# Sixteen single loads of the input, and new hand-written orders, in a four-layer attention and gated-MLP kernel

## The chip, the cores and the metric

The kernel runs on one core of a Trainium2 chip, as one launch. The metric is the device time of that launch in microseconds. Before the change the median of three runs is 380.31 us (379.89 to 380.41). The profile that is read here is of one execution of its own, which took 380.59 us; from its first to its last instruction it spans 378.9 us.

The core has five instruction queues that run side by side and meet only through semaphores: TensorE (PE, with its weight loads as PEld), VectorE (DVE), ScalarE (ACT), GpSimd (POOL) and SyncE (SP), which here does nothing but start DMAs.

## The reference

The input x has 2048 tokens of 448 bf16 values. Four layers follow each other, A, B, A, B, each on the layer-normed x and added back to it. Both A layers use the same weights, and so do both B layers.

```python
def _A_ref(x, wqkv, wo):            # 16 heads of 28
    W, dil = 8, 2
    qkv = (x @ wqkv) -> q, k, v     # split by head
    idx = pos[:, None] - off[None, :]          # 8 keys: the token itself and every second one behind it
    logits = einsum(q, k[idx]) * Dh ** -0.5    # masked where idx < 0
    o = einsum(softmax(logits), v[idx])
    return o @ wo
def _B_ref(x, w_gate, w_up, w_down):           # 1792 hidden values
    return ((x @ w_gate) * (x @ w_up)) @ w_down
x = x + _A_ref(_layernorm(x), A_wqkv, A_wo)
x = x + _B_ref(_layernorm(x), B_w_gate, B_w_up, B_w_down)
x = x + _A_ref(_layernorm(x), A_wqkv, A_wo)
x = x + _B_ref(_layernorm(x), B_w_gate, B_w_up, B_w_down)
```

## The kernel before, in words

**Tiling.** x lies in `x_sb` as 16 blocks of 128 tokens; even tokens are blocks 0 to 7 and odd tokens blocks 8 to 15, so that the dilated window becomes a plain window of 8 neighbours. Each layer is cut into chunks of 256 or 512 tokens, and the chunks of the four layers are interleaved (`SEQ`): a chunk of a later layer starts as soon as its tokens are through the earlier one. Matmuls contract over 64 rows and run two at a time on the two halves of the array; the pair is recorded at L355, and its 32-column variant, which is woven between attention matmuls, at L358.

**The start, which the change touches.** A block of x is loaded (L450), its statistics are taken on DVE (`bn`, L592, and `mv`, L594), ACT makes 1/std in two steps (`lnv`, L595, and `rstd`, L597), DVE writes the normalised block (`xn`, L616), and PE transposes it (`Tps`, L631 or L635) into PSUM, from where ACT or DVE copies it (`T`, L642 and L645). Blocks 14 and 15 of the first layer go through a DMA transpose instead (L624). The qkv weights come in three groups: the V weights `WV`, four stage pieces of the Q and K weights (rows of `hT`, which serves as staging space here), and two small pieces `stv` for a packed layout. Eight copies (`wqk`, L517, on DVE or ACT) spread the stage pieces into `WQK`, and every Q/K matmul waits for all eight. After the last Q/K matmul of tokens 0 to 767 four more copies (`wqp`, L525) fill the gaps of `WQK` with V columns, and the Q/K matmuls of the other tokens wait for them. PE runs 18 matmuls on zeros (L509) while it waits for the first data. The evictions of Q/K results (`QK`, L730) and of V results (`V`, `VT`, L795 to L822) may stand on ACT or on DVE.

**What sets the order.** Nothing is scheduled on the chip or by a planner at build time. The table `ORDER` lists for each of the five queues the numbers of the operations in the order in which they are issued (an entry such as `504*2.4.5/475:1+316:2` is an attention operation with pieces of two others woven in), and `BANKS` gives each PE operation its PSUM banks. An operation waits for the semaphores of its producers and for the release of its banks. Which of two engines runs an eviction is also set by the list in which its number stands. `plain_dma` (L450) adds one DMA on SP; `load_x(q, lo, hi)` adds the load of blocks 4q+lo to 4q+hi-1 as one DMA:

```python
def load_x(q, lo=0, hi=4, tag="", prio=0.0):
    two, b0 = q // 2, 4 * (q % 2)
    plain_dma("sp", x_sb[:, 4 * q + lo:4 * q + hi, :], x_par[two][:, b0 + lo:b0 + hi, :], ...)
```

**The MLP weights.** `WGU` holds the gate weights (`wg`) in rows 0 to 63 and the up weights (`wu`) in rows 64 to 127, each loaded in six pieces of which each waits for the one before it. The MLP's pairs compute a gate product and an up product at once (`Gps`); ACT copies the gate half (L1013), DVE multiplies (L1019), and the down product (`Dd`) is added to x (L980). In layers 1 and 3 the transposes are DMA transposes on SP (L621), which the first MLP matmuls wait for.

Of the kernel before, what the change touches and what calls it, by code (L numbers as in the profile page):

```python
# [15 lines left out]
NCH = S // 512  # L16
# [81 lines left out]
def grp_nc(g):  # L98
# [21 lines left out]
    ),  # L120
    "act": (
# [10 lines left out]
    ),  # L132
    "dve": (
# [1028 lines left out]
```

## Time and profile before

| what | us |
|---|---|
| median of three runs | 380.31 |
| the profiled execution | 380.59 |
| its span | 378.9 |
| PE busy | 373.2 (99%) |
| DVE busy | 271.6 (72%) |
| ACT busy | 199.3 (53%) |
| first matmul on real weights starts at | 8.56 |
| first Q/K matmul starts at | 11.86 |
| first MLP matmul starts at | 50.05 |

PE is counted as busy from the start of a matmul to its modelled end, so a busy PE can still be a little slower than its best. The granted TensorE clock is 1.00 in every stretch that was read. A row of the timeline view gives start, length, engine, line, operation, what it writes and reads, shape, how many instructions were merged, and in brackets the idle time before it with what ended it. "SPq" rows are issues of DMAs, not transfers. A group row of the profile gives busy time and mean ns of one, then the engine's idle time before these instructions.

### The profile page before, as it was taken

How to read it: one execution, taken by the hardware profiler on the slowest of the kernel's cores; microseconds unless marked ns; L12 is line 12 of the kernel's file. 1: busy time of each engine (PE TensorE's matmuls, PEld its weight loads, DVE VectorE, ACT ScalarE, POOL GpSimd, SP SyncE). 2: the span in 40 equal slices, each digit the busy share in tenths (PEclk: the TensorE clock that was granted, in tenths of full speed). 3: DMA queues.
4: the chain of work that ended last, by engine and by line, in shares of the span. 5: the costliest groups of instructions: out<-in, count | busy, mean ns of one | idle time of the engine just before them, and what ended most of it. 6: DMA issues, size and time to landing. Idle time of an engine off the chain costs nothing.

```text
span 378.9 us, 14223 instructions
## 1 busy us (share of the span) xinstructions
PE 373.2 (99%) x6372; PEld 208.2 (55%) x6372; DVE 271.6 (72%) x564; ACT 199.3 (53%) x333; POOL 5.2 (1%) x25
## 2 busy tenths in 40 slices
PE   8999999999999999999999999999999999999997
PEld 3554678544544445455766756554455454444864
DVE  6999989988786385867477978528897587275233
ACT  4898786657444565444466413556766544123310
POOL 5000000000000000000000000000000000000000
DMA  7767464610414023022102125220026104103002
GB/s 248 179 139 150 55 185 132 111 23 21 82 22 69 5 55 72 20 48 55 24 10 52 39 43 100 49 51 21 20 32 95 39 3 90 44 2 74 2 13 98
DMA packets 59892, 24.38 MB, mean 64 GB/s; under 512 B 49016, under 2 KB 59704, under 8 KB 59832
## 3 DMA queue, kind: packets, MB, share of 16 engines
q1 hardware_dynamic: 59688, 23.42, 29.0%
q8 instruction: 50, 0.82, 0.9%
q14 instruction: 10, 0.08, 0.1%
q10 hardware_dynamic: 144, 0.06, 0.1%
HBM read 9.04 MB, written 3.50 MB: 33 GB/s over the span
## 4 chain that ended last, share of the span: by engine, by line
PE 92%; ACT 4%; DMA 2%; SPq 1%; DVE 1%; issue 0%; DVEq 0%
PE ps L355 84%; PE ps L358 4%; PE ps L855 2%; ACT qk L730 2%; PE ps L889 2%; DMA hT<-in_A_wqkv_dram 2%; PE ps L1031 1%; SPq L450 1%; ACT E_sb L864 1%; ACT v_sb L822 0%; ACT R_sb L919 0%; ACT R_sb L920 0%; ACT O_sb L900 0%; DVE WQK L517 0%; DVE Qz L841 0%
## 5 line engine op out<-in xcount | busy, mean ns | idle before, releaser
L355 PE MATMUL ps<-xnTb,WGU 64*128 64x512 bf16 (+1 forms) x1902 | 171.6, 332 | 0.8 <-ACT R_sb L920 0.8
L355 PEld LDWEIGHTS ps<-xnTb,WGU 64*128 64x128 bf16 x1902 | 92.2, 94 | 70.3 <-issue 1.5
L1013 ACT ACTIVATE g_sb<-ps 128x512 bf16<-128x512 f32 x112 | 65.8, 596 | 90.7 <-PE ps L355 86.4
L1019 DVE TENSOR_TENSOR hT<-g_sb,ps 128x512 bf16<-128x512 bf16 x112 | 75.1, 681 | 40.1 <-ACT g_sb L1013 38.8
L355 PE MATMUL ps<-WD,hT 64*128 64x448 bf16 x786 | 80.5, 349 | 0.0
L980 DVE TENSOR_TENSOR x_sb<-x_sb,ps 128x448 bf16<-128x448 bf16 x62 | 36.3, 615 | 30.1 <-PE ps L355 29.8
L355 PEld LDWEIGHTS ps<-WD,hT 64*128 64x128 bf16 x786 | 37.7, 94 | 33.7 <-DVE hT L1019 0.2
L355 PE MATMUL ps<-xnTa,WQK 64*128 64x512 bf16 (+1 forms) x496 | 52.6, 353 | 0.5 <-DVE WQK L517 0.2
L864 ACT ACTIVATE E_sb<-ps,shift_sb 128x1024 bf16<-128x1024 f32 (+1 forms) x36 | 37.2, 1068 | 11.7 <-PE ps L855 11.7
L592 DVE BATCH_NORM_STATS2 st<-x_sb 128x6 f32<-128x448 bf16 x64 | 38.2, 618 | 1.4 <-DMA x_sb<-in_A_x_dram 1.2
L355 PEld LDWEIGHTS ps<-xnTa,WQK 64*128 64x128 bf16 x496 | 22.7, 94 | 22.6 <-DVE O_sb L904 1.0
L730 ACT ACTIVATE qk<-ps 128x1024 bf16<-128x1024 f32 (+1 forms) x28 | 25.4, 931 | 17.5 <-PE ps L355 17.1
L616 DVE TENSOR_SCALAR xn_sb<-x_sb,mv,rstd 128x512 bf16<-128x512 bf16 (+1 forms) x64 | 27.6, 455 | 4.9 <-ACT rstd L597 4.9
L871 DVE TENSOR_TENSOR E_sb<-E_sb,MK 128x1024 bf16<-128x1024 bf16 (+1 forms) x36 | 23.4, 658 | 9.0 <-ACT E_sb L864 8.9
L355 PE MATMUL ps<-wo_g,oT 64*128 64x448 bf16 x151 | 26.0, 350 | 0.0
L355 PE MATMUL ps<-WV,xnTa 64*128 64x336 bf16 (+3 forms) x244 | 23.6, 304 | 0.4 <-DMA WV<-in_A_wqkv_dram 0.4
L919 ACT ACTIVATE R_sb<-R_sb 128x960 f32<-128x960 f32 (+1 forms) x18 | 17.3, 961 | 11.4 <-DVE R_sb L918 11.4
L918 DVE STREAM_SHUFFLE R_sb<-O_sb 128x960 f32<-128x960 f32 (+1 forms) x18 | 21.2, 1180 | 0.0
L900 ACT ACTIVATE O_sb<-ps 128x448 f32<-128x448 f32 (+2 forms) x27 | 13.9, 548 | 11.5 <-PE ps L889 11.3
L939 DVE TENSOR_TENSOR oT<-O_sb,R_sb 128x960 bf16<-128x960 f32 (+1 forms) x16 | 17.5, 1095 | 3.2 <-ACT R_sb L920 3.2
L595 ACT ACTIVATE lnv<-mv,eps_sb 128x2 f32<-128x2 f32 (+1 forms) x33 | 9.2, 292 | 20.0 <-DVE mv L594 17.7
L920 ACT ACTIVATE R_sb<-R_sb 128x960 f32<-128x960 f32 (+1 forms) x18 | 17.3, 959 | 0.3
(67 smaller groups left out, 243.2 us busy)
## 6 DMA issues: line engine op xcount, KB each, us to landing
out_dram<-x_sb SPq DMA_DIRECT2D x15, 112.0 KB, 1.8
x_sb<-in_A_x_dram SPq DMA_DIRECT2D x3, 448.0 KB, 7.4
hT<-in_A_wqkv_dram SPq DMA_DIRECT2D x4, 224.0 KB, 5.5
WGU<-in_B_w_gate_dram SPq DMA_DIRECT2D x4, 224.0 KB, 4.1
WGU<-in_B_w_up_dram SPq DMA_DIRECT2D x4, 224.0 KB, 3.8
WD<-in_B_w_down_dram SPq DMA_DIRECT2D x2, 448.0 KB, 4.2
mv_rows<-oT SPq DMA_DIRECT2D x12, 64.0 KB, 1.7
oT<-mv_rows SPq DMA_DIRECT2D x48, 8.0 KB
```

The costliest lines, as they stand in the source:

```text
L355: return lambda E: E.matmul(out(), lhs(), rhs(), start=start, stop=stop)
L592: sc.add("dve", one(lambda E, B=B: E.bn_stats(st6[:, B, :], x_sb[:, B, :]), ("bn", li, B)), 525.0, deps=[("x", li - 1, B)] + ([("xn", li - ...
L616: sc.add("dve", one(lambda E, B=B, dst=dst, src=src: E.tensor_scalar(dst, src, mv[:, B, 0:1], rstd[:, B:B + 1], ALU.subtract, ALU.mult), ( ...
L730: return E.activation(dst, src, ACT.Copy) if hasattr(E, "activation") else E.tensor_copy(dst, src)
L864: return E.activation(E_sb[:, slot, 2 * hp:2 * hp + 2, 0:w], ps[:, b0:b0 + 2, 0:w], ACT.Exp, bias=shift_sb[:, 0:1], scale=SCALE)
L871: return E.tensor_tensor(e, e, MK[:, kind, 0:nc].unsqueeze(1).unsqueeze(1).to_broadcast([128, 2, w // nc, nc]), ALU.min)
L918: sc.add("dve", one(lambda E: E.stream_shuffle(R, Of, [DH] * 32), ("Rs", li, qb)), dve_est(w) + 20.0, deps=[("Oa", li, g)] + prev, prio=prio)
L919: sc.add("act", one(lambda E: E.activation(R, R, ACT.Ln), ("Rl", li, qb)), act_est(w, False), deps=[("Rs", li, qb)], prio=prio)
L939: return E.tensor_tensor(dst, O.rearrange("p d h n -> p h d n"), Rv.rearrange("p d h n -> p h d n"), ALU.mult)
L980: sc.add("dve", one(lambda E: E.tensor_tensor(x_sb[:, B, :], x_sb[:, B, :], ps[:, bk[w], 0:D], ALU.add), ("x", li, B)), dve_est(D), deps=[ ...
L1013: sc.add("act", one(lambda E, gs=gs, bk=bk: E.activation(g_sb[:, gs, :], ps[:, bk[0], :], ACT.Copy), ("G", li, j, f0)), act_est(512), deps ...
L1019: return E.tensor_tensor(hT[:, f0:f0 + nf, hs, 0:nt], v(g_sb[:, gs, :]), v(ps[:, bk[1], :]), ALU.mult)
```

## The change

The input is loaded by sixteen DMAs of one block (112 KB) each; before, there were two of one block, one of two and three of four. The order on SP becomes x blocks 0, 1, 2, 3, 5, 4, 6, 7, then the V weights, then the four stage pieces as before, then block 15, the first gate piece, and blocks 13, 14, 9, 8, 11, 10, 12. Before, the order after the stage pieces was blocks 12 to 15, the first gate piece, blocks 8 to 11. The operations get new numbers (ten more DMAs stand at the front of the list), and `ORDER` and `BANKS` are new throughout: some evictions change between ACT and DVE, and positions change on every engine but POOL. No arithmetic is added or taken away. The tables are cut to their first lines here; what their numbers mean at the places that count is shown below the diff.

```diff
 ORDER = {
     "pe": (
-        "41 42 43 44 45 46 47 48 49 50 51 52 53 54 112 115 55 56 57 58 211 130 212 133 139 241 136 242 205 235 206 236 229 201 230 203 231 202 157 232 199 154 "
+        "51 52 53 54 55 56 57 58 59 60 61 62 63 122 64 65 66 67 125 68 140 221 222 143 251 149 146 252 215 245 216 246 239 211 167 240 241 212 213 242 164 209 "
...
-    sem_names += ["d_x0g", "d_x0h"]
+    sem_names += [f"d_x{q}{t}" for q in range(NCH) for t in "ghi"]
...
     load_x(0, 0, 1, prio=-51.0)
     load_x(0, 1, 2, "g", -49.6)
-    load_x(0, 2, 4, "h", -49.5)
+    load_x(0, 2, 3, "h", -49.5)
+    load_x(0, 3, 4, "i", -49.5)
...
-    load_x(1, prio=-49.3)
+    for i in range(4):
+        load_x(1, i, i + 1, "_ghi"[i] if i else "", -49.3)
...
     for q in range(2, NCH):
-        load_x(q, prio=-48.5 + 0.5 * (q - 2))
+        for i in range(4):
+            load_x(q, i, i + 1, "_ghi"[i] if i else "", -48.5 + 0.5 * (q - 2))
```

On SP, from the start of the program, before. `hT` stands for the stage pieces (and, in the last row, for the two small pieces of V columns).

```order
L450 DMA x_sb<-in_A_x_dram 128x448 x2
L450 DMA x_sb<-in_A_x_dram 128x2x448
L450 DMA x_sb<-in_A_x_dram 128x4x448
L450 DMA WV<-in_A_wqkv_dram 128x2x448 x2
L450 DMA hT<-in_A_wqkv_dram 128x896 x4
L450 DMA x_sb<-in_A_x_dram 128x4x448
L450 DMA WGU<-in_B_w_gate_dram 64x2x896
L450 DMA x_sb<-in_A_x_dram 128x4x448
L450 DMA WGU<-in_B_w_gate_dram 64x2x896
L450 DMA WGU<-in_B_w_up_dram 64x2x896
L450 DMA hT<-in_A_wqkv_dram 128x2x112 x2
```

The same place with the change:

```order
L452 DMA x_sb<-in_A_x_dram 128x448 x8
L452 DMA WV<-in_A_wqkv_dram 128x2x448 x2
L452 DMA hT<-in_A_wqkv_dram 128x896 x4
L452 DMA x_sb<-in_A_x_dram 128x448
L452 DMA WGU<-in_B_w_gate_dram 64x2x896
L452 DMA x_sb<-in_A_x_dram 128x448 x7
L452 DMA WGU<-in_B_w_gate_dram 64x2x896
L452 DMA WGU<-in_B_w_up_dram 64x2x896
L452 DMA hT<-in_A_wqkv_dram 128x2x112 x2
```

Eight issues instead of four stand ahead of the V weights, and nine instead of three between the stage pieces and the second gate piece. The rest of SP's list keeps its order until the layer-0 results are stored for the packed V.

On DVE, from the copies of the Q/K weights to the normalisation of block 7, before (L517 `wqk`, L592 `bn`, L594 `mv`, L616 `xn`):

```order
L517 COPY WQK<-hT 128x16x28
L616 TENSOR_SCALAR xn_sb<-x_sb,mv,rstd 128x512 x2
L517 COPY WQK<-hT 128x16x28 x7
L592 BN_STATS st<-x_sb 128x6 x2
L594 BN_AGGR mv<-st 128x2 x2
L592 BN_STATS st<-x_sb 128x6 x3
L616 TENSOR_SCALAR xn_sb<-x_sb,mv,rstd 128x512
```

The same place with the change (L809 and L814 are the eviction of the first V result, which stood on ACT; L522 is `wqk`, L597 `bn`, L599 `mv`, L621 `xn`):

```order
L522 COPY WQK<-hT 128x16x28
L621 TENSOR_SCALAR xn_sb<-x_sb,mv,rstd 128x512 x2
L522 COPY WQK<-hT 128x16x28 x6
L597 BN_STATS st<-x_sb 128x6 x2
L599 BN_AGGR mv<-st 128x2
L597 BN_STATS st<-x_sb 128x6
L809 CAST v_sb<-ps 128x8x28
L814 CAST v_sb<-ps 128x4x28
L599 BN_AGGR mv<-st 128x2
L597 BN_STATS st<-x_sb 128x6
L599 BN_AGGR mv<-st 128x2
L621 TENSOR_SCALAR xn_sb<-x_sb,mv,rstd 128x512
```

One `wqk` copy has gone to ACT, and two casts have come from there. The last row of both lists is `xn` of block 7. Ahead of it stood `bn` of blocks 6, 7, 15, 13 and 14; now stand `bn` of blocks 7, 15, 6 and 9.

On PE, from the first Q/K matmul, before (L635 is a block's transpose):

```order
L355 MATMUL ps<-xnTa,WQK 128x256 x6
L355 MATMUL ps<-xnTa,WQK 128x512 x6
L355 MATMUL ps<-xnTa,WQK 128x256 x8
L355 MATMUL ps<-xnTa,WQK 128x512 x14
L355 MATMUL ps<-xnTa,WQK 128x256 x6
L355 MATMUL ps<-xnTa,WQK 128x512 x8
L355 MATMUL ps<-xnTa,WQK 128x256 x6
L355 MATMUL ps<-xnTa,WQK 128x512 x6
L355 MATMUL ps<-xnTa,WQK 128x256 x8
L635 MATMUL ps<-hT,xn_sb 128x64 x8
```

The same place with the change:

```order
L357 MATMUL ps<-xnTa,WQK 128x256 x6
L357 MATMUL ps<-xnTa,WQK 128x512 x6
L357 MATMUL ps<-xnTa,WQK 128x256 x8
L357 MATMUL ps<-xnTa,WQK 128x512 x14
L357 MATMUL ps<-xnTa,WQK 128x256 x6
L640 MATMUL ps<-hT,xn_sb 128x64 x8
```

The first transpose in this stretch, of block 7, stands behind 40 Q/K matmuls instead of behind 68.

More of the change, by code (lines that the diff above doesn't have):

```diff
@@ L106 @@
     "pe": (
[13 rows of a table removed]
[13 rows of a table added]
     ),
     "act": (
[10 rows of a table removed]
[10 rows of a table added]
     ),
     "dve": (
[15 rows of a table removed]
[16 rows of a table added]
     ),
     "pool": (
-        "18 19 38 20 21 22 23 24 25 26 27 28 29 30 31 32 33 34 35 36 37"
+        "28 29 48 30 31 32 33 34 35 36 37 38 39 40 41 42 43 44 45 46 47"
     ),
     "sp": (
[6 rows of a table removed]
[7 rows of a table added]
     ),
```

114 rows, old and new, of tables (BANKS, ORDER) are left out of this document.

## The prediction

> **What bounds the kernel now.** The page's busy table comes first, because it says which engine can set the end at all.
>
> ```profile
> PE   8999999999999999999999999999999999999997
> PE 373.2 (99%) x6372; PEld 208.2 (55%) x6372; DVE 271.6 (72%) x564; ACT 199.3 (53%) x333; POOL 5.2 (1%) x25
> ```
>
> TensorE is busy in nearly every slice, so a change that leaves the matmuls as they are can gain only what PE idles or waits. The windows view splits that by stage: to the first V product, to the first Q/K product, to the attention scores of tokens behind the first 768, to the first MLP product, and the rest.
>
> ```profile
> 0.00:8.56 8.56, 6.89 (x27) 2.73 (x28) 6.27 (x20) 3.73 (x11) 5.20 (x25) 1.00 0.76 237
> 8.56:11.86 3.30, 3.06 (x60) 1.80 (x61) 2.47 (x12) 2.62 (x7) 0.00 (x0) 1.00 1.07 316
> 11.86:22.34 10.48, 10.23 (x160) 5.89 (x161) 9.89 (x38) 8.79 (x21) 0.00 (x0) 1.00 0.64 148
> 22.34:50.05 27.71, 26.69 (x610) 15.13 (x611) 25.87 (x56) 24.14 (x36) 0.00 (x0) 1.00 0.60 121
> 50.05:378.90 328.85, 326.36 (x5516) 182.67 (x5516) 227.14 (x443) 160.02 (x262) 0.00 (x0) 1.00 0.24 50
> ```
>
> After its length, a row has the busy time and count of PE, PEld, DVE, ACT and POOL, then the clock, the DMA share and GB/s. Two things stand out. Behind 50.05 us PE lacks 2.49 us of 328.85. And from 11.86 to 22.34 DVE is busy for 9.89 of 10.48 us: there it is as much the bound as PE. The timeline of PE shows what ends its waits at the start and at 50.05.
>
> ```profile
> 8.56 0.46 PE L355 MATMUL ps<-WV,xnTa 64*128 64x224 bf16 x6 [0.42 <-DMA WV<-in_A_wqkv_dram]
> 10.72 0.94 PE L355 MATMUL ps<-WV,xnTa 64*128 64x448 bf16 x8
> 11.86 5.73 PE L355 MATMUL ps<-xnTa,WQK 64*128 64x256 bf16 x68 [0.20 <-DVE WQK L517]
> 17.43 0.28 PE L635 MATMUL ps<-hT,xn_sb 64*128 64x64 bf16 x8
> 50.05 0.40 PE L355 MATMUL ps<-xnTb,WGU 64*128 64x256 bf16 x4 [0.81 <-ACT R_sb L920]
> ```
>
> PE waits 0.42 us for the V weights, 0.20 us for the last `wqk` copy, and 0.81 us before the first MLP product. That one reads `xnTb` and no `R_sb`, so the engine named is not its producer; the DMA transpose is:
>
> ```profile
> 44.77 1.58 SPq L621 DMA_TRANSPOSE xnTb<-xn_sb  x1
> xnTb<-xn_sb SPq DMA_TRANSPOSE x1, 5.0
> ```
>
> Issued at 44.77, it landed 5.0 us later, at 49.8.
>
> **The change part by part.** *Landings of the weights.* The SP rows of the start, then the landing times of single issues from the DMA view:
>
> ```profile
> 0.80 1.85 SPq L450 DMA_DIRECT2D x_sb<-in_A_x_dram  x4
> 2.70 1.02 SPq L450 DMA_DIRECT2D WV<-in_A_wqkv_dram  x2
> 3.76 1.91 SPq L450 DMA_DIRECT2D hT<-in_A_wqkv_dram  x4
> 5.71 0.65 SPq L450 DMA_DIRECT2D x_sb<-in_A_x_dram  x1
> 7.21 0.59 SPq L450 DMA_DIRECT2D x_sb<-in_A_x_dram  x1
> 13.73 0.60 SPq L450 DMA_DIRECT2D WGU<-in_B_w_gate_dram  x1
> x_sb<-in_A_x_dram SPq DMA_DIRECT2D x2, 112.0 KB, 2.1
> hT<-in_A_wqkv_dram SPq DMA_DIRECT2D x1, 224.0 KB, 5.9
> x_sb<-in_A_x_dram SPq DMA_DIRECT2D x1, 448.0 KB, 7.4
> x_sb<-in_A_x_dram SPq DMA_DIRECT2D x1, 448.0 KB, 7.6
> ```
>
> An x issue takes 1.85/4 = 0.46 us of SP. Four more stand ahead of the weights, so the last stage piece (the 5.9 row, fourth of its group) is issued at about 5.2 + 4 x 0.46 = 7.1 instead of 5.2. It does not have to land later by that much: single blocks landed after 2.1 us, this piece after 5.9, so it spent some 3.8 us in a queue. The rate decides:
>
> ```profile
> 3.00:4.00 1.00, 1.00 (x2) 1.00 0.79 214
> 5.00:6.00 1.00, 1.00 (x3) 1.00 1.08 350
> ```
>
> One block per 0.46 us is 115 KB / 0.46 = 250 GB/s: more than moves between 3 and 4 us, less than the 350 behind 5 us. New x issues hold the stream at 250 until about 6 us, so some 0.1 MB is missing there (a third of a microsecond), while 672 KB of late traffic (four x blocks are still whole now, and 224 KB of gate weights) can no longer run ahead beside the stage pieces in one lump. Bounds for the last piece's landing: 1.8 us later if every DMA kept its latency; earlier without limit, but PE can use little (below). I take no change, being nearest to the row in which the queue moves 350 GB/s. The six other issues come behind the stage pieces, where SP stands idle now from 7.80 to 13.73; 6 x 0.46 = 2.8 us fit in.
>
> The Trainium skill (DMA: Bandwidth & Descriptors, section "Rules for kernel authors") says to coalesce many small transfers; its section "Anatomy of one DMA" puts a fixed 2.0 us on each. Paid one after the other, ten more DMAs would cost 20 us by it. The two 112 KB rows agree with the size of that latency (2.1) and not with paying it in series, since they were issued 0.46 us apart and each landed after 2.1.
>
> *The copies of the Q/K weights.* DVE now does three behind the last stage piece, with the change two (one of the eight goes to ACT, whose nearest row is a Q/K eviction of 0.60 us; ACT has 0.68 us without work in the 3.30 of this stage).
>
> ```profile
> 9.98 1.00 DVE L517 COPY WQK<-hT 128x448 bf16<-128x448 bf16 x4
> 11.16 0.65 DVE L517 COPY WQK<-hT 128x448 bf16<-128x448 bf16 x3 [0.18 <-DMA hT<-in_A_wqkv_dram]
> 13.52 0.60 ACT L730 ACTIVATE qk<-ps 128x512 bf16<-128x512 f32 x1
> ```
>
> Four take 1.00 and three 0.65, so a further copy adds 0.19 (0.65 less one of 0.27, halved): **-0.19 us**, first Q/K product at 11.67. PE is then free: its V products end at 10.72 + 0.94 = 11.66, and one transpose leaves this stretch for the time before 8.56. With earlier weights PE gains at most that transpose and the two waits, under 0.8 us in all.
>
> *Block 7's transpose, 28 matmuls earlier.* It stood at 17.43, far behind its input; now it stands behind 40 of the 68 matmuls, half of them narrow as in the 68: (17.43 - 11.86) x 40/68 = 3.28 us after the first, at 14.95. Its input `xn` of block 7 follows on DVE by these rows:
>
> ```profile
> 11.72 1.14 DVE L592 BATCH_NORM_STATS2 st<-x_sb 128x6 f32<-128x448 bf16 x2
> 12.78 0.30 DVE L594 BATCH_NORM_AGGREGATE mv<-st 128x2 f32<-128x6 f32 x2
> 14.74 0.40 DVE L616 TENSOR_SCALAR xn_sb<-x_sb,mv,rstd 128x512 bf16<-128x512 bf16 x1
> 30.94 0.38 DVE L795 CAST v_sb<-ps 128x224 bf16<-128x224 f32 x1
> 13.12 0.29 ACT L595 ACTIVATE lnv<-mv,eps_sb 128x2 f32<-128x2 f32 x1 [1.04 <-DVE mv L594]
> 14.01 0.20 ACT L597 ACTIVATE rstd<-lnv 128x2 f32<-128x2 f32 x1
> ```
>
> Copies from 11.16 to 11.54, three statistics at 0.54 from start to start, two `mv` at 0.13, the two casts 0.5 (the second is half as wide): 11.54 + 1.62 + 0.26 + 0.50 = 13.9. Then `lnv`, `rstd` and handovers, 0.6: 14.5, while DVE does block 9's statistics until 14.6. `xn` ends at 15.0, so PE stands for about 0.1 us, with the second halves of four Q/K products queued behind: **+0.10 us**. The cover is gone here: every delay of DVE behind 11.16 now reaches PE.
>
> *DVE up to the `wqp` copies at 21.8.* It loses a `wqk` copy (0.19) and two transposed-block copies (0.33 each from start to start), and gains the casts (0.5) and one Q/K eviction of 128x512:
>
> ```profile
> 19.14 0.39 DVE L645 COPY xnTa<-ps 128x512 bf16<-128x512 bf16 x1
> 20.67 0.62 DVE L841 TENSOR_SCALAR Qz<-qk,qmask 128x512 bf16<-128x512 bf16 x2 [0.28 <-ACT qk L730]
> 21.80 0.49 DVE L525 COPY WQK<-hT 128x96 bf16<-128x96 bf16 x4
> 37.23 0.69 DVE L730 CAST qk<-ps 128x512 bf16<-128x512 f32 x1 [0.26 <-PE ps L355]
> ```
>
> That is 0.5 + 0.6 - 0.85 = +0.25 us of work into 0.28 us of idle before `Qz`: **0**. The four `wqp` copies, 0.49 us, then hold the next Q/K products as now.
>
> *To 50.05.* PE's order hardly changes, and block 0's path to the transpose issue is as long as now. **0**, with bounds from the landing: the sixteen such transposes took 3.9 to 5.4 us (median 4.2 on the page), so -0.8 (all of the wait) to +0.4.
>
> ```profile
> DMA to landing us min/median/max: 3.9/4.2/5.4
> ```
>
> *Behind 50.05.* The same number of matmuls, the same numbers woven in. PE lacks 2.49 us there, in pieces that no row gives to one cause; pieces that are ready change places. I take **0**; a gain above 0.5 would need a fifth of all that is lacking, and I allow 0.5 of loss for new waits.
>
> Sum: -0.19 + 0.10 = -0.09 us on the profiled execution's 380.59 (span 378.9 and 1.69 around it). That execution lies 0.28 over the median of the runs, 380.31, so the forecast for the runs is **380.2 us**.
>
> **The rivals.** What a measurement can tell from no change is about 0.2%, 0.76 us; A is my forecast, within it.
>
> *B, faster.* With smaller pieces in the queue the V weights and the stage pieces land 0.4 us earlier or more, and the transpose takes its median 4.2. For it: the 0.42 and 0.20 us waits, the 0.81 wait. Against it: DVE's full stretch gives back what PE gains. 0.2 to 0.4 + 0.8 gives about 1.1: 379.2.
>
> *C, slower: block 9 on DVE.* `bn` of block 9 now stands ahead of `xn` of block 7, and PE's next transpose behind that. Block 9 follows the gate piece and three blocks; by the 3.7 us that 1120 KB took now from the last stage piece (11.1) to the last x block (7.21 + 7.6 = 14.8), its 672 KB give 13.35, and DVE wants it at 13.95. If it lands as late as block 9 does now, 14.8, DVE stands 0.85 us, and so does PE at the transpose: 380.2 + 0.85 = 381.1, and 381.4 with the gate piece's slower stream on top. It decides once block 9 lands later than 2.9 us behind the last stage piece.
>
> *D, slower: the weights follow their issue.* If the queue has drained by 7 us, the last stage piece keeps its 5.9 us less little: up to 12.9, and PE stands up to 1.8 - 0.19 = 1.6 us longer: 381.8. It decides once the piece lands later than 11.3. Against it: the 3.8 us of queueing. The skill's rule on coalescing is on this side.
>
> **How the numbers follow.** A 0.46, B 0.32, C 0.12, D 0.10. Faster by over 0.2% is B, 0.32; slower is C and D, 0.22; within is A, 0.46. The range reaches to B's time and nearly to C's: 379.2 to 381.3. A alone would be 379.6 to 380.9.
>
> **What would show it.** Right: the first Q/K product starts at 11.5 to 11.8, ended by `wqk`; PE's wait at block 7's transpose is under 0.2 us; the next Q/K products behind `wqp` start at 22.2 to 22.4; the first MLP product at 49.9 to 50.1, ended by the DMA transpose; the stretch from there takes 328.4 to 329.3 us. Wrong: an idle row on DVE before `bn` that names x at 12 to 15 us (C), a first Q/K product behind 12.2 (D), one before 11.4 or an MLP start before 49.5 (B), or a stretch behind it that differs by more than 0.5 us, which none of the four explains.

## The result, and the profile after

The change made the kernel slower: the median of six runs is 382.6 us (382.07 to 384.25), that of the kernel before beside it 380.1; the ratio is 1.0078 with a 95% interval of 1.0053 to 1.0102. Run again later, the changed kernel gave 1.0090 (1.0063 to 1.0117). By the medians that is 2.5 and 3.2 us of loss, and the forecast of 380.2 us, with a range up to 381.3, was wrong. The profiled execution took 383.14 us, its span 381.4, against 380.59 and 378.9 before. Three single executions of kernels below (990.5 us of e2, 674.85 of e5, 645.33 of e16) stand in their medians but in no ratio; e5 was traced in its one, so the table has no trace of it.

The page's busy table says that PE does the same work and waits more (98% where it was 99%); 8 us of evictions have gone to DVE, 4 us less are on ACT:

```profile
PE 373.7 (98%) x6372; PEld 208.5 (55%) x6372; DVE 279.5 (73%) x572; ACT 195.0 (51%) x325; POOL 5.2 (1%) x25
```

The windows view of the changed kernel, cut at the same events as before (first V product, first Q/K product, scores behind the first 768 tokens, first MLP product), with the same columns:

```profile
0.00:9.16 9.16, 6.80 (x34) 2.68 (x35) 6.64 (x21) 4.08 (x11) 5.18 (x25) 1.00 0.72 201
9.16:13.21 4.05, 2.87 (x53) 1.69 (x53) 2.37 (x10) 3.19 (x7) 0.00 (x0) 1.00 1.06 276
13.21:23.66 10.45, 10.21 (x161) 6.11 (x162) 10.12 (x39) 8.30 (x19) 0.00 (x0) 1.00 0.63 158
23.66:51.06 27.40, 26.76 (x610) 15.10 (x611) 24.93 (x53) 24.15 (x36) 0.00 (x0) 1.00 0.54 111
51.06:381.40 330.34, 327.09 (x5516) 182.87 (x5516) 235.43 (x452) 155.28 (x255) 0.00 (x0) 1.00 0.24 51
```

Against 8.56, 3.30, 10.48, 27.71 and 328.85 us the stages took +0.60, +0.75, -0.03, -0.31 and +1.49. Two places lose: the time to the first Q/K product (+1.35 together), and the stretch behind the first MLP product. PE's timeline shows the waits:

```profile
9.16 1.08 PE L357 MATMUL ps<-WV,xnTa 64*128 64x224 bf16 x14 [1.11 <-DMA WV<-in_A_wqkv_dram]
13.21 3.44 PE L357 MATMUL ps<-xnTa,WQK 64*128 64x256 bf16 x40 [0.95 <-DVE WQK L522]
16.49 0.28 PE L640 MATMUL ps<-hT,xn_sb 64*128 64x64 bf16 x8
51.06 3.23 PE L357 MATMUL ps<-xnTb,WGU 64*128 64x256 bf16 x56 [0.41 <-DMA xnTb<-xn_sb]
77.83 3.20 PE L357 MATMUL ps<-xnTb,WGU 64*128 64x512 bf16 x28 [0.70 <-DMA xnTb<-xn_sb]
```

PE waits 1.11 us for the V weights (0.42 before) and 0.95 for the last copies of the Q/K weights (0.20). What the copies wait for is the landing of the stage pieces, which can be read from SP's timeline and the DMA view (issue to landing) of the same execution: the issues of the x blocks, the V weights, the stage pieces and the first gate piece, then the landing of six single blocks and of the last stage piece alone.

```profile
0.80 3.73 SPq L452 DMA_DIRECT2D x_sb<-in_A_x_dram  x8
4.57 0.95 SPq L452 DMA_DIRECT2D WV<-in_A_wqkv_dram  x2
5.56 1.89 SPq L452 DMA_DIRECT2D hT<-in_A_wqkv_dram  x4
7.97 0.76 SPq L452 DMA_DIRECT2D WGU<-in_B_w_gate_dram  x1
x_sb<-in_A_x_dram SPq DMA_DIRECT2D x6, 112.0 KB, 2.5
hT<-in_A_wqkv_dram SPq DMA_DIRECT2D x1, 224.0 KB, 5.6
```

The last stage piece is issued at 7.02 us (the fourth of the 5.56 row) instead of 5.23 and takes 5.6 us instead of 5.9: it lands at 12.58 instead of 11.13. It kept its time in the queue and lost 1.45 of the 1.8 us of the later issue. The single blocks, on the other hand, land 2.5 us after their issue, hardly more than the 2.1 of the first two before, so little is queued when the weights are issued. The windows view from 2 to 7 us, before and then after, has less moved in the last column (GB/s); the column before it, the DMA engines' busy share, falls only from 0.96 to 0.88, so they aren't idle, but move less while busy:

```profile
2.00:7.00 5.00, 5.00 (x19) 2.04 (x18) 3.77 (x13) 1.10 (x6) 3.88 (x17) 1.00 0.96 285
```

```profile
2.00:7.00 5.00, 5.00 (x20) 1.93 (x18) 4.18 (x14) 1.68 (x8) 3.85 (x17) 1.00 0.88 228
```

That is 5 us x 57 GB/s = 0.285 MB less moved by 7 us, or 0.8 us at the 350 GB/s that the kernel before reaches behind 5 us.

### The profile page after: what moved, and what is told of

Read it like the earlier page. It is cut to its first block, busy times and chain, and to the rows that moved or that the text cites. A ratio compares the mean times of both kernels' runs of the same rounds, so it can differ in the third digit from the quotient of the medians.

```text
span 381.4 us, 14235 instructions
## 1 busy us (share of the span) xinstructions
PE 373.7 (98%) x6372; PEld 208.5 (55%) x6372; DVE 279.5 (73%) x572; ACT 195.0 (51%) x325; POOL 5.2 (1%) x25
## 4 chain that ended last, share of the span: by engine, by line
PE 89%; DMA 4%; DVE 3%; SPq 1%; ACT 1%; issue 1%
PE ps L357 81%; PE ps L360 3%; DMA xnTb<-xn_sb 3%; PE ps L894 2%; PE ps L860 2%; SPq L452 1%; DMA hT<-in_A_wqkv_dram 1%; PE ps L1036 1%; DVE xn_sb L621 0%; DVE R_sb L923 0%; ACT E_sb L869 0%; DVE E_sb L876 0%; DVE x_sb L985 0%; DVE O_sb L905 0%; DVE st L597 0%
## 5 line engine op out<-in xcount | busy, mean ns | idle before, releaser
L597 DVE BATCH_NORM_STATS2 st<-x_sb 128x6 f32<-128x448 bf16 x64 | 38.1, 614 | 0.9 <-DMA x_sb<-in_A_x_dram 0.7
L621 DVE TENSOR_SCALAR xn_sb<-x_sb,mv,rstd 128x512 bf16<-128x512 bf16 (+1 forms) x64 | 27.8, 456 | 4.5 <-ACT rstd L602 4.1
L735 ACT ACTIVATE qk<-ps 128x1024 bf16<-128x1024 f32 (+1 forms) x24 | 22.3, 935 | 15.0 <-PE ps L357 14.9
L905 ACT ACTIVATE O_sb<-ps 128x448 f32<-128x448 f32 (+3 forms) x23 | 12.0, 548 | 17.1 <-PE ps L894 17.1
```

What stands on the lines that cost most here:

```text
L597: sc.add("dve", one(lambda E, B=B: E.bn_stats(st6[:, B, :], x_sb[:, B, :]), ("bn", li, B)), 525.0, deps=[("x", li - 1, B)] + ([("xn", li - ...
L621: sc.add("dve", one(lambda E, B=B, dst=dst, src=src: E.tensor_scalar(dst, src, mv[:, B, 0:1], rstd[:, B:B + 1], ALU.subtract, ALU.mult), ( ...
L735: return E.activation(dst, src, ACT.Copy) if hasattr(E, "activation") else E.tensor_copy(dst, src)
```

## The experiments

All loads are named by their blocks; "|" stands ahead of the V weights and stage pieces and behind them, "g" is the first gate piece. "Old" and "new" orders are those of the kernel before and of the change. This table gives, of each traced execution, when the last stage piece landed (issue plus the time in the DMA view), when the first Q/K and the first MLP product started (PE's timeline), and what of the span lies behind the latter.

```
kernel                              last piece  Q/K    MLP    behind  ratio to before
before                                11.13    11.86  50.05  328.8
the change                            12.58    13.21  51.06  330.3   1.0078 (1.0053-1.0102)
e14 the change again                  12.21    12.84  50.72  329.5   1.0090 (1.0063-1.0117)
e1  loads only, old orders            12.01    12.74  50.70  329.7   1.0023 (1.0003-1.0042)
e3  head split only, old orders       11.84    12.57  50.72  329.0   1.0052 (1.0031-1.0074)
e13 loads only, g second              12.49    13.22  51.36  329.7   1.0070 (1.0051-1.0088)
e4  late split only                   10.08    10.81  49.16  328.8   1.0009 (0.9985-1.0032)
e16 late split, g last                10.14    10.87  48.19  329.8   1.0003 (0.9989-1.0016)
e17 late split, g second              10.63    11.39  50.29  328.8   1.0019 (1.0000-1.0037)
e2  new orders, coarse loads          10.32    11.88  49.84  330.0   1.0028 (1.0006-1.0050)
e18 the change, coarse head loads      9.74    11.68  49.48  329.5   1.0033 (1.0021-1.0044)
e9  the change, g last                12.08    12.71  50.31  329.5   1.0046 (1.0030-1.0062)
e10 new head, old tail, coarse loads  10.17    11.46  49.45  329.9   1.0052 (1.0031-1.0073)
e15 the same again                     9.71    11.56  49.14  330.3   1.0058 (1.0039-1.0077)
e7  old head, new tail, coarse loads  10.25    10.98  48.89  329.9   1.0024 (1.0006-1.0041)
e6  new head, old tail, new loads     13.11    13.75  51.72  330.3   1.0071 (1.0043-1.0098)
e5  the change, one transpose back       (no usable trace)           1.0072 (1.0048-1.0096)
e8  head split, four loads on ACT     10.10    12.49  51.17  328.9   1.0036 (1.0021-1.0050)
e11 coarse, three loads on ACT         9.41    13.03  51.06  328.8   1.0041 (1.0023-1.0059)
e12 coarse, blocks 4 to 7 on ACT       9.66    11.93  50.67  328.8   1.0017 (0.9998-1.0036)
```

**The loads against the orders.** Four kernels take the change apart. My theory by now was that every load ahead of the weights delays them; the rival, that the new orders cost the time.

```diff
 e1: orders of before, loads split in place
-x0 x1 x2-3 x4-7 | | x12-15 g x8-11
+x0 x1 x2 x3 x4 x5 x6 x7 | | x12 x13 x14 x15 g x8 x9 x10 x11
 e2: ORDER and BANKS of the change, loads as before
 e3: orders of before
+x0 x1 x2 x3 x4 x5 x6 x7 | | x12-15 g x8-11
 e4: orders of before
+x0 x1 x2-3 x4-7 | | x12 x13 x14 x15 g x8 x9 x10 x11
```

> The kernel before with its x loads split in place into one-block DMAs (same order of the blocks, same order of all other work). Theory 'stream': every further DMA ahead of the weights costs the stream about 0.25 us, so the last stage piece lands near 12.5 us instead of 11.1, the first Q/K product starts at 13.0 to 13.4, and the time is 380.1 + 1.3 = 381.4 us. Theory 'orders' (the new orders of the engines cost the time, the loads cost nothing): last stage piece at 11.1 to 11.4, time 379.9 to 380.4.

> The changed kernel with the coarse loads of before (blocks 2-3, 4-7, 12-15 and 8-11 together, at the places of before): the new orders alone. Theory 'stream': last stage piece at 11.1, first Q/K product at 11.6 to 11.8; what remains is the late DMA transpose of the second MLP chunk (0.7 to 0.9 us) and perhaps 0.85 us of DVE waiting for block 9: 380.8 to 381.6 us. Theory 'orders': 382.3 us or more, as the change. If neither the transpose nor block 9 costs: 380.0.

> The kernel before with only blocks 2 to 7 split (four more DMAs, all ahead of the weights); the late blocks stay whole. Theory 'stream': nearly all of the loss of the loads-only kernel: first Q/K product at 12.8 to 13.3, 381.2 us. Rival 'late mixing' (the late single blocks slow the stage pieces that share the queue with them): first Q/K product below 12.1, 380.1 to 380.4.

> The kernel before with only blocks 8 to 15 split (six more DMAs, all behind the stage pieces). Theory 'stream': stage pieces land as before (11.1), first Q/K product at 11.8 to 12.0, 380.1 us. Rival 'late mixing': last stage piece at 12 or later, 381 us.

Measured: 380.92, 381.49, 381.73 and 379.88 us (medians; before 379.92). The head split alone is slower (e3: 1.0052), the late split is not (e4). e1 lies between its two cases and below e3, though all of e3's loads stand ahead of its weights; the first gate piece, which e1 issues 1.7 us later than e3, comes up again below. The rows of PE at the first Q/K product, of e3 and of e4:

```profile
12.57 5.73 PE L356 MATMUL ps<-xnTa,WQK 64*128 64x256 bf16 x68
```

```profile
10.81 5.73 PE L356 MATMUL ps<-xnTa,WQK 64*128 64x256 bf16 x68
```

In every traced kernel with the old head orders and all loads on SP the first Q/K product starts 0.73 to 0.76 us behind the last stage piece; in all kernels the first MLP product follows 37.3 to 38.9 us behind the first Q/K product. But the orders are not free either: e2, with its stage pieces as early as 10.32, is 1.0028, and both theories are right in part. In e2 PE starts Q/K at 11.88, 1.56 behind the last piece, and then shows both waits that its expectation names, though smaller. DVE waits for block 9 (0.20 us), and the second DMA transposes are late:

```profile
14.33 0.63 DVE L593 BATCH_NORM_STATS2 st<-x_sb 128x6 f32<-128x448 bf16 x1 [0.20 <-DMA x_sb<-in_A_x_dram]
76.27 3.19 PE L356 MATMUL ps<-xnTb,WGU 64*128 64x512 bf16 x28 [0.27 <-DMA xnTb<-xn_sb]
```

**Issue or size of the loads.** Are the weights late because SP issues them later, or because more DMAs keep the DMA engines longer? e8 keeps the DMAs of e3 and lets ACT issue four of them.

```diff
 e8: orders of before, late blocks whole
-SP: x0 x1 x2 x3 x4 x5 x6 x7 | | x12-15 g x8-11
+SP: x0 x1 x2 x3 | | x12-15 g x8-11
+ACT: x4 x5 x6 x7, then its table load
```

> The head-split kernel (order of before, blocks 2 to 7 one by one) with the loads of blocks 4 to 7 issued by ACT at its start instead of by SP: the same number and size of DMAs, but the weights' issues stand as early as before. Theory 'issue' (the weights land later because SP issues them later): last stage piece at 10.2 to 11.2, first Q/K product at 11.0 to 11.9, time 379.5 to 380.2. Rival 'cost per DMA' (every further DMA keeps the 16 DMA engines about 0.25 us, whoever issues it): last piece near 12, 381.3 to 381.8 as with the head split.

The last stage piece landed at 10.10, not 11.84: the same bytes in the same pieces, but issued early. So it is the issue: between e3 and e8 the piece is issued 1.82 us earlier and lands 1.74 us earlier. From 2 to 7 us the same pieces move at 234 GB/s in e3 and at 289 in e8 (windows view, e3 then e8):

```profile
2.00:7.00 5.00, 4.94 (x23) 2.06 (x22) 4.17 (x14) 1.79 (x9) 3.81 (x17) 1.00 0.88 234
```

```profile
2.00:7.00 5.00, 4.78 (x13) 1.61 (x11) 2.16 (x8) 2.00 (x5) 3.68 (x17) 1.00 0.97 289
```

The time still was 1.0036, for the reason that its expectation left out: x itself. Rows of ACT's queue, the DMA view and PE:

```profile
0.80 1.85 ACTq L451 DMA_DIRECT2D x_sb<-in_A_x_dram  x4
x_sb<-in_A_x_dram SPq DMA_DIRECT2D x3, 112.0 KB, 4.0
7.87 0.85 PE L636 MATMUL ps<-hT,xn_sb 128*128 128x128 bf16 x8 [1.09 <-DVE xn_sb L621]
12.49 5.72 PE L356 MATMUL ps<-xnTa,WQK 64*128 64x256 bf16 x68
```

With a second queue at work, blocks 1 to 3 on SP (the row of three, median) took 4.0 us from issue to landing, block 0 landed at 3.36 instead of 2.9, DVE began late, and PE waited for `xn` instead of for weights. e11 and e12 use the finding for a faster kernel: the coarse kernel with large DMAs on ACT's queue.

```diff
 e11: kernel before
+ACT: x4-7, the first two stage pieces, then its table load (taken from SP)
 e12: kernel before
+ACT: x4-7, then its table load (taken from SP)
```

> The kernel before (coarse loads, its orders) with blocks 4 to 7 (one DMA) and the first two stage pieces issued by ACT at its start, so that large DMAs are in flight from 1 us on. Theory 'issue': the last stage piece lands at 8.5 to 9.5 and the first Q/K product starts at 10.0 to 11.0, if DVE is not late; each us there is a us at the end: 378.8 to 379.6. Against it, as in the run with four blocks on ACT: blocks 0 and 1 land 0.5 us later or more, DVE starts later, and the first Q/K product is at 12 or more: 380.5 to 381.5.

> The kernel before with only blocks 4 to 7 (one DMA) issued by ACT at its start: the weights' issues stand 0.5 us earlier on SP. Theory 'issue': last stage piece 0.3 to 0.6 us earlier, first Q/K product at 10.5 to 11.3, 379.4 to 380.0 us; if blocks 0 to 3 land later by 0.5 us and more, as with the four on ACT, 380.3 to 381.0.

Both miss the gain and hit the warning (e11, at 381.66 us, a little beyond it): the last piece lands at 9.41 and 9.66, earlier than in any other kernel, and the first Q/K product starts at 13.03 and 11.93. Block 1 of e12 on SP, beside the 448 KB on ACT:

```profile
x_sb<-in_A_x_dram SPq DMA_DIRECT2D x1, 112.0 KB, 3.8
```

The Trainium skill (DMA: Bandwidth & Descriptors, section "Queues, rings and completion order") says that a DMA engine goes round the queues that have work for it, a packet from each. These runs agree that the queues share the engines: 3.8 us for a block beside another queue's large load, where it took 2.1 before with one queue. That they change by packets, no run here shows. Its section "Rules for kernel authors" adds that spreading DMAs over engines saves issue time and no more; that too is what e8 and e12 show, where the weights came earlier by what SP had saved and x came later.

**Head and tail.** The new orders up to the first MLP product ("head") and behind it ("tail") were joined with the old ones, the cut taken from the trace.

```diff
 e5: the change, on SP
-T.1.2+3, VT.0.10, VT.0.12, T.1.4+5
+T.1.2+3, T.1.4+5, VT.0.10, VT.0.12
 e6: ORDER, BANKS: head of the change, tail of before; one-block loads
 e7: head of before, tail of the change; coarse loads
 e10, e15: head of the change, tail of before; coarse loads
```

> The changed kernel with one row of SP's order put back: the DMA transpose of the second MLP chunk's blocks (T.1.4+T.1.5) stands again right behind that of the blocks before it, ahead of two transposes of V. Theory 'late transpose': the wait of 0.70 us that PE has at 77.8 us goes, time 382.6 - 0.8 = 381.8 us. Rival (that wait is only one run's slow transfer): 382.4 to 382.8.

> The changed kernel up to its first MLP product, and behind it the order of before on all engines (with one-block loads). Theory 'head and tail apart': the head costs about 1.2 us (first MLP product at 50.8 to 51.2), the stretch behind it is that of before (328.7 to 329.3 us): 381.2 to 381.5 us. If the loss behind 50 us came from the head (work carried over), the stretch stays at 330 and the time at 382.4 or more.

> The kernel before (coarse loads, its orders) up to its first MLP product, and behind it the order of the change on all engines. Theory 'head and tail apart': first MLP product at 49.5 to 50.1, stretch behind it 329.8 to 330.3 us, time 380.8 to 381.3 us. If the new orders behind 50 us cost nothing by themselves: 379.9 to 380.3.

> Coarse loads, the orders of the change up to the first MLP product, the orders of before behind it: the cell that is missing between before, loads alone, head alone and tail alone. Theory 'additive': the new head by itself costs what its wait for block 9 costs, 0.2 to 0.4 us: 380.2 to 380.5 us. Theory 'the new head costs 1.7 us whatever the loads': 381.7.

> The new head with coarse loads and the old tail, once more. Its first trace (the fastest of its runs) had the first MLP product at 49.45 us and 0.75 us of waiting for the down weights behind it. If a usual run differs in the head: first MLP product at 50.0 or later; if it differs behind it: a stretch above 330. Time 381.5 to 382.3.

Measured: 383.15, 383.15, 380.9, 382.01 and 381.76 us. e7 (1.0024, a stretch of 329.9) and e15 (330.3) came as expected in time and stretch but not at the first MLP product; e6 came as its second case says (382.4 or more, a stretch of 330); e5 and e10 missed. Putting the transpose back (e5) gained nothing, and the 0.70 us wait at 77.83 comes and goes: e2 and e7, with the same tail, wait 0.27 and 0.26 us there, e9 and e18 not at all. The second trace of the change passes the place without a wait, and its stretch takes 329.45:

```profile
50.72 3.23 PE L357 MATMUL ps<-xnTb,WGU 64*128 64x256 bf16 x56 [0.43 <-DMA xnTb<-xn_sb]
50.72:380.17 329.45, 326.94 (x5516) 182.89 (x5516) 235.12 (x452) 155.20 (x255) 0.00 (x0) 1.00 0.24 51
```

And e6 was not cheaper than the change, though its tail is the old one. The old tail has a wait of its own that comes and goes: its first down product sometimes waits for the down weights. PE, SP and the DMA view of e1:

```profile
67.47 1.50 PE L357 MATMUL ps<-WD,hT 64*128 64x448 bf16 x14 [0.60 <-ACT g_sb L1025]
62.73 0.37 SPq L452 DMA_DIRECT2D WD<-in_B_w_down_dram  x1
WD<-in_B_w_down_dram SPq DMA_DIRECT2D x1, 336.0 KB, 4.5
```

The row names ACT, but the piece issued at 62.73 landed at 67.27, 0.20 us before PE went on. Traces with the old tail have 328.8 to 329.0 us behind the first MLP product without this wait (before, e3, e4, e8, e11, e12, e17) and 329.7 to 330.3 with one of 0.6 to 0.9 us (e1, e6, e10, e13, e15, e16; all three traces that join the new head to the old tail have it); those with the new tail 329.5 where nothing is late (e9, e14, e18) and 329.9 to 330.3 with a late transpose. So the new tail is 0.6 us slower than the undisturbed old one and about equal to the disturbed one; that is why the parts don't add up. No wait carries the 0.6: PE is busy 326.94 us for the same 5516 matmuls that took 326.36. Which pieces are woven into the attention work did change, as the groups of narrow gate and up pieces show (before, and the change):

```profile
L358 PE MATMUL ps<-xnTb,WGU 64*32 64x512 bf16 x232 | 9.4, 378 | 0.0
```

```profile
L360 PE MATMUL ps<-xnTb,WGU 64*32 64x512 bf16 x208 | 8.6, 378 | 0.0
```

Whether that is where the 0.6 lies is open.

e10 and e15 were slower in the runs (1.9 and 2.4 us above before) than in their traces (spans 0.4 and 0.5 above that of before). Most of this is which execution was traced: theirs (381.25 and 381.4 us) lie 0.76 and 0.36 us below their medians, and the one of before (380.59) lies 0.5 and 1.2 above the medians beside them (380.1 and 379.35). The other 0.3 us lies outside the span: time less span is 1.9 to 2.0 us in every execution of e6, e10 and e15, and 1.7 to 1.8 in those of all other kernels. Why that is so isn't shown.

**The gate piece.** In the change the first gate piece is second behind the stage pieces.

```diff
 e9: the change
-x15 g x13 x14 x9 x8 x11 x10 x12
+x15 x13 x14 x9 x8 x11 x10 x12 g
 e13: e1
-x12 x13 x14 x15 g x8 x9 x10 x11
+x12 g x13 x14 x15 x8 x9 x10 x11
 e14: the change, unchanged
 e16: e4, g behind x11;  e17: e4, g behind x12
 e18: the change, with x2-3 and x4-7 together
```

> The changed kernel with the first gate piece moved behind all late blocks on SP; nothing else moves. Theory 'gate' (the gate piece, second behind the stage pieces, spreads the 16 DMA engines and delays the last stage piece beyond what the later issue costs): last stage piece at 11.8 to 12.1 as in the two kernels with the order of before (12.01, 11.84), first Q/K product at 12.4 to 12.8, time 381.6 to 382.0 us. Rival 'scatter' (12.58 and 13.11 were only slow samples): time as the change, 382.4 to 383.1.

> The loads-only kernel (all blocks single, orders of before) with the first gate piece second among the late blocks (block 12, gate piece, blocks 13, 14, 15, 8 to 11), as in the change. Theory 'gate': the last stage piece lands at 12.4 to 13.1 instead of 12.0, and the time is 381.0 + 0.5 to 1.0 = 381.5 to 382.0 us. Rival: the gate's place counts only with the new orders: 380.8 to 381.1.

> The changed kernel itself, once more, for a second trace. If the late stage piece is its habit: last piece at 12.4 to 13.1, first Q/K product at 13.0 to 13.8. The wait for the second DMA transposes at 77.8 us (0.70 us) is expected between 0 and 0.9 us, since the gate-last kernel with the same order behind 50 us did not show it. Time 382.3 to 383.2.

> The kernel before with blocks 8 to 15 single and the first gate piece behind all of them; coarse head loads. Theory 'gate': with the gate piece out of the way the stage pieces land at 10.0 to 10.3 each time and the time is 379.3 to 379.9 us, below before by up to 0.6; if before's own gate place (behind four blocks) costs nothing, 379.9 to 380.1.

> The kernel before with coarse head loads, blocks 8 to 15 single and the first gate piece second among them. Theory 'gate by itself': the last stage piece lands 0.4 to 0.8 us later than with the gate piece behind (10.08, 10.14), time 0.5 to 1.3 us above before. Theory 'gate only behind a split head': last stage piece at 10.0 to 10.3, time within 0.3 us of before.

> The change with one thing undone: blocks 2-3 and blocks 4-7 loaded together again (late blocks single, gate piece second, all new orders). If the head loads are the whole loss: ratio to before 1.000 to 1.002, first Q/K product at 11.3 to 11.7. If the new orders cost by themselves as in the run with all loads coarse: 1.002 to 1.004. If the gate piece in second place costs here too: 1.005 or more.

Measured: 381.56, 382.32, 382.56, 379.87, 380.98 and 380.98 us. e9, e17 and e18 came as one of their cases says; e13 came in 0.3 us above its range, e14 in its time but with an earlier last piece (12.21), and e16 showed the stage pieces as expected (10.14) but no gain over before. Behind a split head the place counts: moved last, the change gains (1.0046 against 1.0078 and 1.0090); moved second, the loads-only kernel loses (1.0070 against 1.0023, no overlap), and these loads, under the old orders, are nearly the whole loss of the change. The rows of PE of e9 and e13:

```profile
12.71 3.44 PE L357 MATMUL ps<-xnTa,WQK 64*128 64x256 bf16 x40 [0.24 <-DVE WQK L529]
```

```profile
13.22 5.73 PE L357 MATMUL ps<-xnTa,WQK 64*128 64x256 bf16 x68 [0.77 <-DVE WQK L529]
```

The four traces of the table with the gate piece second behind single head blocks (the change, e14, e13, e6) have the last stage piece at 12.21 to 13.11, the three with it further back at 11.84 to 12.08. But e5, whose issues on SP are the change's up to there, had it at 11.77 in its traced execution, so the landings alone don't settle it; the times of e13 and e1 do. With a coarse head there is no such order (9.74 and 10.63 second, 9.71 to 11.13 further back), and e16, e17 and e4 can't be told apart by their intervals. The DMA engines' own landings of the last stage piece, from the trace's completion events, show what differs (first, median and last of the 16 engines):

```
before      9.31   9.65  11.13        the change  10.20  10.83  12.58
e18         9.32   9.49   9.74        e14         10.34  10.52  12.21
e16         9.32   9.59  10.14        e13         10.21  10.74  12.49
```

The median engine is 0.9 to 1.3 us later in the right column than in the left, less than the 1.8 us of later issue; the last one is another 1.7 to 1.8 behind it, where it is 0.2 to 0.6 behind in e18 and e16 (1.5 in the one trace of before). Single head blocks with the gate piece further back (e1, e3, e9) have 1.0 to 1.3, so a part of the spread is the split head's own. Why a gate piece that is issued behind the stage pieces should widen that spread isn't shown. e3, whose gate piece stands behind one DMA of four blocks but is issued just as early (8.0 us), lies between e1 and e13 (1.0052); so it may be the time of its issue that counts, not its rank. And the half microsecond at the first Q/K product is less than the 1.2 to 1.8 us that the times show. Part of that is again the traced execution: e1's, of 382.09 us, was the longest of its twelve, 1.2 above their median, and e13's lay 0.5 above. The rest isn't seen in the traces.

e18 sums it up: with two DMAs instead of six for blocks 2 to 7, the change is at 1.0033. The head loads are worth 0.0045 to 0.0057 of 380 us, 1.7 to 2.2 us, under the new orders; under the old ones they are worth 0.0051 (e13 against e17). Neither pair's intervals overlap. The 0.0033 left in e18 is not the new orders alone, since e17, with the old orders and late blocks that differ only in their sequence, has 0.0019. So the orders are worth 0.0014 there and 0.0008 to 0.0020 behind a split head (the change against e13), 0.3 to 0.8 us, which these intervals don't tell from nothing; with all loads coarse (e2) they cost 0.0028. e18's Q/K products start at 11.68, though its stage pieces are there at 9.74. PE is not held by weights there:

```profile
10.80 0.29 PE L642 MATMUL ps<-hT,xn_sb 64*128 64x64 bf16 x8 [0.16 <-DVE WQK L524]
11.68 1.59 PE L356 MATMUL ps<-xnTa,WQK 64*128 64x256 bf16 x20
```

e4, with the old head, starts them at 10.81: the new head costs 0.7 to 0.9 us there (e7 has 10.98) if the weights come early, and nothing if they come late. At the first MLP product little of it is left: 49.14 to 49.84 in the four traces with a new head and early weights, 48.19 to 50.29 in the four with the old one. The new tail adds its 0.6 against the undisturbed old one. No kernel beat the one before: e4, e16 and e12 can't be told from it.

## Why the prediction was wrong

*Landings of the weights: 0.* This is the step that failed, and the bounds had it (a landing 1.8 us later). I saw that the last stage piece lay 3.8 us in a queue and concluded that a later issue would shorten its stay. It stayed 5.6 us instead of 5.9. By an estimate from SP's rows, the queue that a stage piece stands in is mostly made of the weights issued just before it: 224 KB each 0.5 us, about 460 GB/s, more than the 350 to 380 that were moved. With the change that queue starts later and from little, since the single blocks, one each 0.47 us, hardly fill it (they land 2.0 to 2.9 us after their issue). I estimated 0.1 MB missing "until about 6 us"; 0.285 MB were missing by 7. Landing: +1.45 us in one trace, +1.08 in the other. That also shows a flaw in the basis: the one trace of before, with 11.13, was the latest of the nine with coarse head loads on SP. Against the other eight (9.71 to 10.63) the change's last piece lands 1.6 to 2.9 us later, for 1.8 us of later issue.

*Copies: -0.19.* Measured -0.10: the first Q/K product follows the last piece after 0.63 us in the change's traces and 0.73 in those of the old orders. *Block 7's transpose: +0.10.* It stood where I had put it, 3.28 us behind the first Q/K product (16.49), and did not wait: 0. *DVE up to `wqp`: 0.* Right: the stage took 10.45 instead of 10.48. *To 50.05: 0, with -0.8 to +0.4.* Right: -0.31, with the wait for the transpose at 0.41 instead of 0.81.

*Behind 50.05: 0 with 0.5 either way.* Wrong in size: +1.49 and +0.60 in the two traces. 0.6 belongs to the new order (e9, e14 and e18 agree), and 0.70 more was a late second transpose, which I had not looked for. Two V transposes went ahead of it on SP; that these made it late isn't shown, since putting it back ahead of them (e5) gained nothing. "The same numbers woven in" was not so (208 narrow gate and up pieces instead of 232). And the 2.49 us that PE "lacks" there were misread as pieces that could be won or lost. In the kernel before, whose span is 378.9 us, PE's last products end at 376.47:

```profile
370.97 5.50 PE L1031 MATMUL ps<-WD,hT 128*128 128x448 bf16 x42
```

So 2.4 us are the end of the kernel, behind the last product, and only about 0.1 us were waits: there was next to nothing to gain.

*The rivals.* D was what happened, at its place and nearly its size: a last piece "up to 12.9" (12.58) and 1.6 us of loss at the first Q/K product (1.35). I gave it 0.10, against it only "the 3.8 us of queueing". Its condition, a queue drained by 7 us, was not quite what happened: the windows view has 325 GB/s from 7 to 8 us, so the stream was nearly full again by then, only later. The Trainium skill's rule on coalescing (DMA: Bandwidth & Descriptors, section "Rules for kernel authors"), which I had put on its side, had the direction; the 2.0 us that the page puts on each DMA of the GpSimd path, paid in series, would have been 20. C didn't come about: block 9 landed at 14.85, as feared, but 2.3 us behind the last stage piece, below its limit of 2.9. In e2 it was 4.0 behind, DVE waited 0.20, and in e10 PE 0.33 at block 7's transpose, less than half of C's 0.85. B's wish, weights 0.4 us earlier, came true only where the head loads were coarse, and there only against a trace of before that was the latest of its kind.

The signs named for a wrong forecast worked: "a first Q/K product behind 12.2" pointed to D, and the stretch that differs by more than 0.5 to a cause that none of the four had.

## What to carry to other kernels

A queue of DMAs behaves by when it fills: ask of each transfer whether the ones ahead of it are large enough to keep the stream at its full rate until it is issued, and if they are not, most of a later issue is a later landing (1.74 of 1.82 us between e8 and e3). Time spent in a queue is slack only if the queue's head stays where it was. And loads that are needed first paid here for a second queue opened beside them, so moving issues to another engine exchanged one late input for another. Last, take the basis of a forecast from several traces: one trace of before put a landing at 11.13 that lay at 9.71 to 10.63 in eight others.

## What was not expected of the hardware

With eight single blocks of 112 KB ahead, one queue moved 228 GB/s between 2 and 7 us, with the mixed sizes of before 285; the first is near what SP puts out in that time (112 KB each 0.47 us, about 240 GB/s), an estimate from its rows. The 16 DMA engines finish the last stage piece 2.4 us apart in the change (10.20 to 12.58) and 0.4 in e18, and the last of them sets the landing. The same kernel's span differs by 1.2 us between two traces (381.4 and 380.2) mostly from landings: the last stage piece, 12.58 and 12.21, and one transpose, which PE waits for 0.70 us or not at all.
